# Sums of blocks of g by adding DMA transfers, and seven-segment products for the first pair of units

## Chip, cores and metric

The kernel runs on one core of a Trainium2 chip. The metric is the device time of one execution in microseconds (us). The engines are PE (TensorE, matrix products), DVE (VectorE), ACT (ScalarE), POOL (GpSimd) and SP (SyncE, which here only issues transfers). Each has its own queue and works through it in order; a DMA transfer is issued by an engine's queue and then runs on its own.

## The reference

A Mamba-2 scan is followed by a two-layer feed-forward block. Only what the change touches is given in full.

```python
# scan: x (4, 8, 768, 32), a (4, 8, 768), B and C (4, 8, 768, 16) -> attn_out (4, 8, 768, 32)
...
x = np.ascontiguousarray(attn_out.transpose(0, 2, 1, 3)).reshape(B * S, H * D)   # (3072, 256)
h = x @ w_in                              # w_in (256, 2048)
g = h * (1.0 / (1.0 + np.exp(-h)))        # silu
return (g @ w_out).astype(np.float32)     # w_out (2048, 256), result (3072, 256)
```

All is in 32-bit floats. The weights come as 64-bit floats and are converted on the chip.

## The kernel before

**Units and pairs.** The 3072 tokens are 12 units of 256. Two units make a pair, P = 0 to 5. For each unit the scan yields XM, the unit's x; the first product and silu yield g (tile gT, in the dictionary GTS, 128 partitions by 16 blocks of 256 tokens); the second product yields the output.

**Products by seven.** From pair 2 on, the first product of two units (f_x1) is made with seven multiplications of blocks in the place of eight (the Strassen-Winograd scheme). It needs sums of blocks of the weights (SW, made by f_SW) and of x (XT, made by f_XT). From pair 1 on, the second product (s2_pair) is made so too: seven segments named 1, w, 5, 6, 7, 4, 3, each of eight matmuls that add up in one bank of PSUM (o_ps), with sums of blocks of w_out (SO, made by f_SO on DVE) and of g (f_TS). The sums of g come in four steps, i = 0 to 3: step 0 writes the tile TN, steps 2, 1 and 3 overwrite blocks b12, b11 and b21 of g in place. Here b12 is the first half of d_ff of the pair's second unit, and so on. Step 1 uses the result of step 2, and step 3 that of step 1. Each step is eight operations of 128x256 on POOL (on DVE in part for the last pair). When a segment ends, ACT copies o_ps into a tile ps; POOL adds ps tiles (p_add); DVE transposes the result and SP issues its four output transfers (f_out). The ps_o pool has one buffer, so the next segment's first matmul waits for ACT's copy.

**Units 0 to 3, and the old list.** In the first product units 0 to 3 are computed directly by f_s1, eight rounds of four matmuls each. In the second product units 0 and 1 are computed directly by s2_list: per unit 32 matmuls.

**The order.** It is written out by hand. Each engine's queue follows the order in which the Python code calls. After the start-up, a stage of eight rounds runs f_s1 for unit 2 with four matmuls of the second product of unit 0 behind each round (f_s2(4)), and then a stage for unit 3 with those of unit 1. The names used later:

- *Pieces.* Weights are converted in 16 pieces, 0 to 7 of w_in and 8 to 15 of w_out: ACT (w_size), DVE (three operations) and POOL (L182, in w_bits). Pieces 13, 14 and 15 are made in rounds 0 to 2 of unit 2's stage ("late").
- *Scan of a unit*, spread over the rounds by scan_piece: P (prefix products, DVE), E (a scan, DVE), T (transposes, DVE), B and C (POOL), G (PE; it needs B), S and M (DVE, after G), SM (ACT, after S), Y (PE) and X (ACT copies the result into XM).
- *Loads of a unit* (load_unit): 17 transfers issued by SP. In unit 3's stage, rounds 2 and 5 issue those of units 6 and 7.
- *Stages of seven products*, G = 2 to 5: eight rounds of f_x1(G), each with the scan of the units two further on and seven matmuls of s2_pair(G - 1). ORDER is a hand-written string for each round: W, 1, 5, 6, 7, 4, 3 are first-product matmuls, s is one second-product matmul. Segment 5 of round 0 needs the first of the four XT differences, which POOL makes (f_XT) at the end of the stage before.
- *Tail.* After stage 5 the second product of the last pair stands alone, s2_pair(5, True).

Of the kernel before, what the change touches and what calls it, by code (L numbers as in the profile page):

```python
# [21 lines left out]
def kernel(  # L22
# [22 lines left out]
    nc = tc.nc  # L45
# [425 lines left out]


    def f_s1(g, j):
        if j == 0:
            GTS[g] = gpool.tile([128, NF, UT], FP32, name="gT")
# [7 lines left out]
        nc.scalar.activation(GTS[g][:, 2 * j:2 * j + 2], hp, AF.Silu)  # L483
# [3 lines left out]

    def s2_list(units):
        for g in units:
            b, t0 = at(g)  # L490
            r = out[b * S + t0:b * S + t0 + UT].rearrange("(k c i) m -> k i c m", k=2, c=2)
            o = ps_o.tile([128, 2, d_model], FP32, name="o_ps")
            for c in range(2):
                for f in range(NF):
                    nc.tensor.matmul(out=o[:, c], lhsT=GTS[g][:, f, 128 * c:128 * c + 128], rhs=w_out_sb[:, f, :],  # L495
                                     start=(f == 0), stop=(f == NF - 1), skip_group_check=True)
                    if f == NF - 1 and c == 1:
                        for e in range(2):
                            o_sb = ppool.tile([128, UT], FP32, name="ps")
                            nc.scalar.activation(o_sb, o[:, e], AF.Copy)  # L500
                            for k in range(2):
                                nc.sync.dma_start(out=r[k][:, e], in_=o_sb[64 * k:64 * k + 64])
                    yield
# [6 lines left out]
    def f_SO(i):  # L510
# [4 lines left out]
        def new():  # L515
            if i == 3:
                return lo(spare(None, 128))
            return [wtp.tile([128, 2, WF], FP32, name=n).rearrange("p a (b m) -> p (a b) m", m=128)
                    for n in ("wu", "wv")]
# [3 lines left out]
        a0, a1, op = ((b(0, 1), b(1, 1), ALU.add), (SO[0], b(0, 0), ALU.subtract),  # L523
                      (b(0, 0), b(0, 1), ALU.subtract), (b(1, 0), SO[min(i, 1)], ALU.subtract))[i]
# [3 lines left out]
    def gb(P, k, v):  # L528

        return GTS[2 * P + v].rearrange("p (j k) t -> p k j t", k=2)[:, k]  # L530

    def f_TS(P, i, q, engine):


        if i == 0 and q == 0:
            TN[P] = tpool.tile([128, NF // 2, UT], FP32, name="TN")
        b11, b21, b12, b22 = gb(P, 0, 0), gb(P, 1, 0), gb(P, 0, 1), gb(P, 1, 1)
        o, a0, a1 = ((TN[P], b12, b11), (b11, b22, TN[P]), (b12, b22, b12), (b21, b21, b11))[i]
        for j in (2 * q, 2 * q + 1):
            engine.tensor_tensor(out=o[:, j], in0=a0[:, j], in1=a1[:, j], op=ALU.subtract)  # L540
# [389 lines left out]
```

## Time and profile before

| What | Value |
|---|---|
| Median of 3 runs | 359.7 us (359.67 to 360.05) |
| Profiled execution: its own time | 358.11 us |
| Profiled execution: span from first to last instruction | 356.3 us |
| PE busy | 344.3 us, 97% of the span |
| DVE, ACT, POOL busy | 183.2, 160.7, 181.9 us |
| PE line L572 (second product by seven), share of the ending chain | 30% in o_ps, 3% in hp |
| PE line L495 (old list) | 128 records, 30.9 us |
| POOL line L540 (f_TS) | 72 + 40 + 32 operations of about 0.745 us |
| POOL line L627 (f_SW) | 4 operations of about 2.35 us |

A 32-bit matmul appears in the trace as two records, so 128 records are 64 matmuls. A busy time of a group is the time in which at least one of its records ran. L is a line of the kernel before. The time of the execution is 1.8 us longer than its span, for what lies ahead of the first and behind the last instruction.

### The profile page before, as it was taken

The numbers are of one execution on the slowest core, as the hardware profiler recorded it, in microseconds if no ns is written. First come the engines' busy times: TensorE is split into PE (matmuls) and PEld (weight loads), VectorE is DVE, ScalarE is ACT, GpSimd is POOL, SyncE is SP. The second block draws the span as 40 slices with busy tenths as digits, with TensorE's granted clock in tenths as the row PEclk, the third lists the DMA queues.
The fourth block names the chain that finished last, engine by engine and source line by source line (L and its number), as shares of the span: only waits on it lengthen the run. The fifth ranks groups of instructions, "written<-read, shape, count | busy, mean of one in ns | idle before, by whom it ended". The sixth has DMA issues, their size and how long they took to land.

```text
span 356.3 us, 8309 instructions
## 1 busy us (share of the span) xinstructions
PE 344.3 (97%) x3276; PEld 289.0 (81%) x3277; DVE 183.2 (51%) x389; ACT 160.7 (45%) x390; POOL 181.9 (51%) x246
## 2 busy tenths in 40 slices
PE   7879999999999999999999999999999999999994
PEld 2457888888888888888888888888888888888883
DVE  7978999554447444643454633455632221214722
ACT  2649575223222545545544545544545454453100
POOL 4434345524059076498274398264398930596100
PEclk9999999999999999999999999999999999999998
DMA  6898966871455270161026253110001010001203
GB/s 118 211 338 139 328 192 113 139 115 50 99 109 76 63 110 7 46 110 29 15 53 108 44 99 42 16 18 2 15 2 18 15 17 0 15 2 20 40 2 45
DMA packets 110059, 26.53 MB, mean 74 GB/s; under 512 B 98884, under 2 KB 105796, under 8 KB 110020
## 3 DMA queue, kind: packets, MB, share of 16 engines
q1 hardware_dynamic: 107044, 25.67, 35.5%
q10 hardware_dynamic: 2976, 0.33, 0.6%
q8 instruction: 26, 0.43, 0.5%
q14 instruction: 13, 0.11, 0.1%
HBM read 22.83 MB, written 3.15 MB: 73 GB/s over the span
## 4 chain that ended last, share of the span: by engine, by line
PE 91%; DVE 4%; DMA 2%; issue 1%; POOL 0%; SPq 0%; ACT 0%; ACTq 0%; DVEq 0%
PE o_ps L572 30%; PE hp L655 28%; PE hp L481 15%; PE o_ps L495 8%; PE hp L572 3%; PE gy L461 3%; PE gy L452 2%; PE gy L398 2%; DVE E L297 1%; PE gy L383 1%; DVE wv L178 1%; DMA tbc<-in_C_dram 1%; DMA tbc<-in_B_dram 1%; DMA out_dram<-ot 0%; DVE gT L273 0%
## 5 line engine op out<-in xcount | busy, mean ns | idle before, releaser
L658 DVE TENSOR_TENSOR gT<-hp,p 128x256 f32<-128x256 f32 x64 | 26.9, 420 | 84.6 <-ACT p L669 47.5
L481 PE MATMUL hp<-XM,w_in_sb 128*128 128x256 f32 x256 | 59.4, 381 | 1.9 <-POOL w_in_sb L182 1.1
L661 ACT ACTIVATE gT<-gT 128x256 f32<-128x256 f32 x96 | 39.7, 413 | 42.8 <-DVE gT L658 42.8
L334 POOL TENSOR_TENSOR BT<-bn,E 128x256 f32<-128x256 f32 x12 | 9.0, 751 | 94.5 <-PE hp L655 29.6
L572 PE MATMUL o_ps<-gT,w_out_sb 128*128 128x256 f32 x224 | 56.5, 379 | 0.0
L481 PEld LDWEIGHTS hp<-XM,w_in_sb 128*128 128x128 f32 x256 | 48.0, 190 | 9.7 <-POOL w_in_sb L182 2.4
L655 PE MATMUL hp<-raw 128*128 128x256 f32 x192 | 52.7, 380 | 0.0
L540 POOL TENSOR_TENSOR gT<-gT 128x256 f32<-128x256 f32 x72 | 51.3, 745 | 0.0
L572 PEld LDWEIGHTS o_ps<-gT,w_out_sb 128*128 128x128 f32 x224 | 42.4, 190 | 5.9
L655 PEld LDWEIGHTS hp<-raw 128*128 128x128 f32 x192 | 36.2, 190 | 5.4 <-POOL ps L543 0.6
L483 ACT ACTIVATE gT<-hp 128x512 f32<-128x512 f32 x32 | 19.1, 596 | 40.1 <-PE hp L481 40.1
L669 ACT ACTIVATE p<-hp 128x256 f32<-128x256 f32 x64 | 24.6, 384 | 27.5 <-PE hp L655 25.7
L658 DVE TENSOR_TENSOR gT<-hp,u 128x256 f32<-128x256 f32 x32 | 13.6, 424 | 40.8 <-PE hp L655 40.8
L655 PE MATMUL hp<-XM,w_in_sb 128*128 128x256 f32 x128 | 34.1, 389 | 0.0
L543 POOL TENSOR_TENSOR ps<-ps 128x256 f32<-128x256 f32 x28 | 20.4, 729 | 26.0 <-ACT ps L579 12.7
L495 PE MATMUL o_ps<-w_out_sb,gT 128*128 128x256 f32 x128 | 30.9, 384 | 0.0
L540 POOL TENSOR_TENSOR TN<-gT 128x256 f32<-128x256 f32 x40 | 28.8, 745 | 0.0
L495 PEld LDWEIGHTS o_ps<-w_out_sb,gT 128*128 128x128 f32 x128 | 23.8, 190 | 3.8 <-issue 0.5
L655 PEld LDWEIGHTS hp<-XM,w_in_sb 128*128 128x128 f32 x128 | 23.3, 190 | 4.3 <-issue 1.0
L297 DVE TENSOR_TENSOR_SCAN E<-ab,diag 128x256 f32<-128x256 f32 (+1 forms) x32 | 24.5, 804 | 3.7 <-PE gy L461 3.4
L540 POOL TENSOR_TENSOR gT<-gT,TN 128x256 f32<-128x256 f32 x32 | 22.2, 743 | 0.0
L579 ACT ACTIVATE ps<-o_ps 128x256 f32<-128x256 f32 x31 | 11.9, 384 | 18.5 <-PE o_ps L572 18.1
(121 smaller groups left out, 543.0 us busy)
## 6 DMA issues: line engine op xcount, KB each, us to landing
ab<-in_a_dram SPq DMA_DIRECT2D x40, 128.0 KB, 3.7
raw<-in_moe_w_in_dram SPq DMA_DIRECT2D x8, 512.0 KB, 8.1
raw<-in_moe_w_out_dram SPq DMA_DIRECT2D x8, 512.0 KB, 6.5
xt<-in_x_dram SPq DMA_DIRECT2D x24, 128.0 KB, 4.1
out_dram<-ot SPq DMA_DIRECT2D x76, 32.0 KB, 1.7
bn<-in_B_dram SPq DMA_DIRECT2D x22, 64.0 KB, 5.1
tbc<-in_C_dram SPq DMA_DIRECT2D x40, 32.0 KB, 2.1
pa<-in_a_dram SPq DMA_DIRECT2D x10, 128.0 KB
```

Of the source, the lines that this page charges most:

```text
L297: nc.vector.tensor_tensor_scan(out=E[u].rearrange("p k h t -> p (k h t)")[:, Q * g0:Q * (g0 + n)], data0=t.rearrange("p g t -> p (g t)"), ...
L481: nc.tensor.matmul(out=hp[:, i], lhsT=w_in_sb[:, kc, f * 128:(f + 1) * 128], rhs=xm[:, kc], start=(kc == 0), stop=(kc == KC - 1))
L483: nc.scalar.activation(GTS[g][:, 2 * j:2 * j + 2], hp, AF.Silu)
L495: nc.tensor.matmul(out=o[:, c], lhsT=GTS[g][:, f, 128 * c:128 * c + 128], rhs=w_out_sb[:, f, :], start=(f == 0), stop=(f == NF - 1), skip_ ...
L540: engine.tensor_tensor(out=o[:, j], in0=a0[:, j], in1=a1[:, j], op=ALU.subtract)
L543: engine.tensor_tensor(out=o, in0=p, in1=q, op=ALU.add)
L572: nc.tensor.matmul(out=o, lhsT=w(j), rhs=g()[:, j], start=(j == 0), stop=(j == NF // 2 - 1))
L579: nc.scalar.activation(pn, on, AF.Copy)
L655: nc.tensor.matmul(out=o, lhsT=w, rhs=x_, start=start, stop=True, skip_group_check=True)
L658: nc.vector.tensor_tensor(out=o, in0=p, in1=q, op=ALU.add)
L661: nc.scalar.activation(o, i, AF.Silu)
L669: nc.scalar.activation(o, i, AF.Copy)
```

## The change

1. *Sums of g's blocks.* g's tile is laid out so that each half of d_ff is contiguous in a partition. Most steps of f_TS become DMA transfers issued by POOL that add to their destination, two halves of 128x1024 (512 KB) per step. TN is first filled by a plain transfer that SP issues (f_TN). All steps are additions now; signs in SO and in the output sums change accordingly. In the tail, DVE and POOL make the second half of steps 0 and 2, and DVE makes steps 1 and 3, in operations of 128x1024.
2. *Pair 0.* s2_list is gone. Pair 0 uses s2_pair with joint=True: its segments 1 and w run together, block by block, in the two halves of one o_ps tile, and then 5, 6, 7, 4 and 3 follow. The rounds of the two stages run 4, 4, 4, 4, 3, 3, 3, 3 and 4, 3, 4, 3, 4, 3, 4, 3 of its 56 matmuls. Pair 0's outputs now go through p_add, transposes and f_out in these stages.
3. *Weight sums.* f_SW runs on DVE, no longer on POOL; f_SO and f_SW stand at other rounds.

The core of the diff (new functions in full):

```diff
+    def new_g():
+        return gpool.tile([128, NF, UT], FP32, name="gT").rearrange("p (k j) t -> p k j t", k=2)
...
-        nc.scalar.activation(GTS[g][:, 2 * j:2 * j + 2], hp, AF.Silu)
+        nc.scalar.activation(GTS[g][:, :, j], hp, AF.Silu)
...
-        a0, a1, op = ((b(0, 1), b(1, 1), ALU.add), (SO[0], b(0, 0), ALU.subtract),
-                      (b(0, 0), b(0, 1), ALU.subtract), (b(1, 0), SO[min(i, 1)], ALU.subtract))[i]
+        a0, a1, op = ((b(0, 1), b(1, 1), ALU.subtract), (SO[0], b(0, 0), ALU.subtract),
+                      (b(0, 0), b(0, 1), ALU.subtract), (b(1, 0), SO[min(i, 1)], ALU.add))[i]
...
+    def f_TN(P, h):
+        if h == 0:
             TN[P] = tpool.tile([128, NF // 2, UT], FP32, name="TN")
+        js = slice(4 * h, 4 * h + 4)
+        nc.sync.dma_start(out=TN[P][:, js], in_=gb(P, 0, 1)[:, js])
+
+    def f_TS(P, i, h, engine=None):
         b11, b21, b12, b22 = gb(P, 0, 0), gb(P, 1, 0), gb(P, 0, 1), gb(P, 1, 1)
-        o, a0, a1 = ((TN[P], b12, b11), (b11, b22, TN[P]), (b12, b22, b12), (b21, b21, b11))[i]
-        for j in (2 * q, 2 * q + 1):
-            engine.tensor_tensor(out=o[:, j], in0=a0[:, j], in1=a1[:, j], op=ALU.subtract)
+        js = slice(4 * h, 4 * h + 4)
+        o, a = ((TN[P], b11), (b11, b12), (b12, b22), (b21, b11))[i]
+        if engine is None:
+            nc.gpsimd.dma_start(out=o[:, js], in_=a[:, js], accum_op=ALU.add)
+        elif i == 0:
+            engine.tensor_tensor(out=o[:, js], in0=a[:, js], in1=b12[:, js], op=ALU.add)
+        else:
+            engine.tensor_tensor(out=o[:, js], in0=a[:, js], in1=o[:, js], op=ALU.add)
...
+        if joint:
+            o = ps_o.tile([128, 2, UT], FP32, name="o_ps")
+            for j in range(NF // 2):
+                for n, (m, w, g) in enumerate(segs[:2]):
+                    nc.tensor.matmul(out=o[:, n], lhsT=w(j), rhs=g()[:, j], start=(j == 0 and n == 0), stop=(j == last),
+                                     skip_group_check=True)
...
-        nc.gpsimd.tensor_tensor(out=t, in0=a0, in1=a1, op=op)
+        nc.vector.tensor_tensor(out=t, in0=a0, in1=a1, op=op)
...
-    S2.append(s2_list((0, 1)))
+    for h in range(2):
+        f_TN(0, h)
+        f_TS(0, 0, h)
+    S2.append(s2_pair(0, joint=True))
     for j in range(8):
+        waiting, PEND[:] = PEND[:], []
         f_s1(2, j)
-        scan_piece(3, j, ("", "", "T", "E", "BS", "G", "S", "Y"))
-        f_s2(4)
+        f_s2(4 if j < 4 else 3)
         if j < len(late):
             w_steps(late[j])
+        scan_piece(3, j, ("", "", "T", "OE", "DCO", "G", "OS", "Y"))
+        outputs(waiting)
         if j in (2, 5):
             load_unit(4 + j // 3)
...
+        for h in range(2):
+            if j in (0, 4, 6):
+                f_TS(0, {0: 2, 4: 1, 6: 3}[j], h)
     for j in range(8):
+        waiting, PEND[:] = PEND[:], []
         f_s1(3, j)
-        scan_piece(4, j, ("TE", "BS", "G", "Y", "", "", "", ""))
-        scan_piece(5, j, ("", "", "T", "E", "BS", "G", "Y", ""))
+        scan_piece(4, j, ("TE", "DCS", "G", "YO", "", "", "", ""))
+        scan_piece(5, j, ("", "", "T", "E", "DCS", "G", "YS", ""))
         scan_piece(6, j, ("",) * 7 + ("t",))
-        f_s2(4)
+        f_s2(4 - j % 2)
+        outputs(waiting)
         if j in (2, 5):
             load_unit(6 + j // 3)
-        if j in (1, 4, 6, 7):
-            f_SO(len(SO))
+        if j == 5:
+            f_TN(1, 0)
+            f_TS(1, 0, 0)
+            f_TS(1, 2, 0)
         if j == 7:
             for i in range(4):
                 f_XT(2, i)
-        if j == 5:
-            sums(1, (0, 1))
     for G in range(2, NU // 2):
         S2.append(s2_pair(G - 1))
...
+        f_TN(G - 1, 1)
         for j, (dve, act, pe) in enumerate(plan):
...
+            if j == 0:
+                f_TS(G - 1, 0, 1)
+                f_TS(G - 1, 2, 1)
+            if j == 1 or j == 3:
+                for h in range(2):
+                    f_TS(G - 1, j, h)
+            if j == 5:
+                f_TN(G, 0)
+                f_TS(G, 0, 0)
+                f_TS(G, 2, 0)
             if j == 6 and more:
                 for i in range(4):
                     f_XT(G + 1, i)
...
     P = NU // 2 - 1
-    sums(P, (3,))
+    f_TS(P, 0, 1, nc.vector)
+    f_TS(P, 2, 1, nc.gpsimd)
...
-            for q in range(4):
-                f_TS(P, 2 * n + 1, q, nc.vector)
+            for h in range(2):
+                f_TS(P, 2 * n + 1, h, nc.vector)
```

"D" and "C" in the new strings are B and C of the scan called singly, "O" is f_SO, "S" is f_SW. outputs calls the output steps that the round before left waiting.

## The prediction

> **What bounds the kernel now.** First the page: busy time, the slices, the chain that ended last. Then one window over PE from its last start-up gap to its last matmul.
>
> ```profile
> PE 344.3 (97%) x3276; PEld 289.0 (81%) x3277; DVE 183.2 (51%) x389; ACT 160.7 (45%) x390; POOL 181.9 (51%) x246
> PE   7879999999999999999999999999999999999994
> PE 91%; DVE 4%; DMA 2%; issue 1%; POOL 0%; SPq 0%; ACT 0%; ACTq 0%; DVEq 0%
> ```
> ```profile
> 27.65:351.40 323.75, 323.75 (x2916) 277.16 (x2916) 160.42 (x340) 148.24 (x366) 170.78 (x223) 1.00 0.33 62
> ```
>
> From 27.65 to 351.40 us PE is busy for all of its 323.75 us. So every matmul removed there is worth its pitch, and every new wait of PE costs its whole length. POOL and DVE are half idle: what they lose or gain counts only where PE, directly or through POOL's or SP's queue, waits for it. The stage that changes most is 55.15 to 116.97 (units 2 and 3 in the first product, 0 and 1 in the second). Its queues, in the timeline by engine:
>
> ```profile
> 113.52 1.89 PE L481 MATMUL hp<-XM,w_in_sb 128*128 128x256 f32 x8
> 115.24 1.89 PE L495 MATMUL o_ps<-w_out_sb,gT 128*128 128x256 f32 x8
> 116.97 1.03 PE L655 MATMUL hp<-XM,w_in_sb 128*128 128x256 f32 x4
> ```
> ```profile
> 57.70 1.38 POOL L182 TENSOR_TENSOR w_out_sb<-wu,wv 128x512 uint32<-128x512 uint32 x1 [0.97 <-DVE wv L178]
> 60.04 1.27 POOL L182 TENSOR_TENSOR w_out_sb<-wu,wv 128x512 uint32<-128x512 uint32 x1 [0.96 <-DVE wv L178]
> 62.74 1.27 POOL L182 TENSOR_TENSOR w_out_sb<-wu,wv 128x512 uint32<-128x512 uint32 x1 [1.42 <-DVE wv L178]
> ...
> 112.47 0.89 POOL L638 TENSOR_TENSOR raw<-XM 128x256 f32<-128x256 f32 x1 [0.24 <-ACT XM L470]
> ```
> ```profile
> 56.94 0.63 SPq L86 DMA_DIRECT2D pa<-in_a_dram  x1
> ...
> 98.53 0.64 SPq L86 DMA_DIRECT2D pa<-in_a_dram  x1
> 99.21 2.85 SPq L115 DMA_DIRECT2D tbc<-in_B_dram  x4
> 102.11 1.83 SPq L115 DMA_DIRECT2D tbc<-in_C_dram  x4
> 104.04 2.65 SPq L95 DMA_DIRECT2D ab<-in_a_dram  x4
> 106.79 1.19 SPq L107 DMA_DIRECT2D bn<-in_B_dram  x2
> 108.08 1.42 SPq L122 DMA_DIRECT2D xt<-in_x_dram  x2
> ```
>
> To see: eight records (four matmuls) start every 1.73 us, so one matmul costs 0.432 us. The w_out pieces 13, 14 and 15 (57.70, 60.04, 62.74) are done 2.4 to 4.2 us before PE reads them. A unit's loads cost SP about 10 us of issue (98.53 to 109.50: 11.0). The x differences for the next stage (L638) are ready 4.4 us before that stage's first seven-product matmul, at 117.83.
>
> **What the Trainium skill says.** "DMA: Bandwidth & Descriptors", section "Anatomy of one DMA — SWDGE (gpsimd) path": about 2.0 us plus bytes/436e3, so for 512 KB an estimated 3.2 us; a semaphore wait happens on the issuing sequencer before dispatch. The profile has 6.5 to 8.1 us for the 512 KB weight loads, with others in flight. The same page, "Latency and other measured facts": a DMA issued from GpSimd (POOL) needs about 1 us to its first byte; I take that as POOL's time per issue. The kernel before has none. "Collectives: The Full Stack", "The bandwidth ceiling: the fold count and why AG ≠ RS ≠ AR": an adding transfer pays for two source reads, not for the add; so I estimate 2.0 + 2 x 1.2 = 4.4 us for 512 KB. Not shown by this trace either. "SBUF — State Buffer", "Who interferes with whom": a DVE operation with two SBUF inputs and a reading GpSimd one exclude each other. The trace agrees: L526 on 128x512 takes 0.67 us alone, 1.13 to 1.21 us beside POOL.
>
> **Part by part.**
>
> 1. *Seven segments for units 0 and 1.* 64 matmuls become 56: 8 x 0.432 = 3.45 us less on PE, all on the path.
>
> 2. *Bank changes.* The pair's o_ps has one buffer. The old list changed it only between rounds. Now segments change inside a run of second-product matmuls three times (5 to 6, 7 to 4, 4 to 3). Evacuation starts 0.04 us after the last matmul's end (83.90, ACT L500 at 83.94), takes 0.384 us (L579), and the next matmul starts some 0.1 us later (estimate): against a pitch of 0.216 after a start, 0.379 + 0.04 + 0.384 + 0.1 leaves 0.7 us lost each. At 7 to 4 ACT first copies XM (0.6 us, after Y): 0.8. At 4 to 3 ACT first runs SM of unit 5, which ends 1.7 us after G (73.53 to 75.28 in unit 3's case), while PE reaches the change 0.86 us after G: 1.3. The first, 5 to 6, is in point 4.
>
> 3. *w_out pieces behind the sums (A).* SP issues the two TN copies where unit 4's loads began, 56.94. With xt ahead of them I put their landing at 61.0 and 62.2 (3.2 us each plus queue). POOL's queue now reads: add into TN half 0, half 1 (each waits for its copy), piece 13, two more adds, pieces 14 and 15. With 1 us per issue: piece 13 done at 64.5, 14 at 67.8, 15 at 69.1. PE wants them at 62.9, then 67.2 and 68.8 in its delayed course: 1.7 + 0.7 + 0.4 = 2.8 us. Bounds: 0.8 (copies by 60.5, issue 0.3) and 6 (weight-load latency).
>
> 4. *First use of a doubly summed block (B).* SO[0] on DVE waits for piece 15; E of unit 3 comes behind it (about 4.7 us), then B and C on POOL (0.7 each), and only then POOL issues b11's add: about 76.2, landed at about 81.1. Segment 6 wants it at 79.7: 1.4 us, the bank change included. Bounds 0.7 and 4.5 (an add of 8 us).
>
> 5. *x differences behind a copy (E).* This is the largest term. In unit 3's round 5 POOL gets the next pair's first adds, ahead of f_XT. They wait for a TN copy on SP, which stands behind unit 7's 17 load issues, and these behind segment 7's output issues, which wait for DVE. From the end of G of unit 4 (T): DVE does S and M (2.6), T (1.1), SO[3] (1.3 to 2.1), P and E0 (1.7), E (2.3), SW[2] (1.2 to 2.0), the transpose (0.4): T+11.4. SP: four output issues 2.5 (L552: 10.25 us for 12 under load, L502: 2.5 for 4), loads 10.0, the copy's issue 0.4: T+24.3; landed T+27.8. POOL: two issues 2.0 (0.6 to 2.4), segment 3's add 0.73, first difference 0.77: T+31.2. PE from T to segment 5 of the next stage: rounds 2 to 7 with points 2's waits, T+24.6. A wait of 6.4 us; bounds 4.3 and 9. Even with SP on time, segment 3's add now stands before f_XT and costs some 1.2 us.
>
> 6. *POOL relieved.* 144 L540 operations (72 + 40 + 32, 102.3 us) and four L627 (9.5 us) leave POOL: nothing for PE, which waited on none of them. In their place stand 42 adds and 11 copies of 512 KB. In the seven-product stages (54 us, eight rounds of 6.7) each sum is due about two rounds after its issue, so 4.4 us hides; it stops hiding at about 10 us. The DMA share there is 0.34, later 0.07; eight adds fit a stage at up to 6.7 us each.
>
> 7. *SW on DVE, SO earlier, signs swapped, g's layout, tail.* DVE is idle for 32% and 51% of the stage's two halves (20.84 busy of 30.69 us, 15.36 of 31.20); beyond points 4 and 5 nothing, and at most the four SW's 5 to 8 us if it were full. In the tail DVE and POOL each do 128x1024 at once (POOL 2.35, L627); segment 5 starts 6.9 us in, the first sums end earlier: nothing. If that cover went, at most 2 us.
>
> Sum: -3.45 + 0.8 + 1.3 + 2.8 + 1.4 + 6.4 = +9.2 us. The profiled execution (span 356.3, its own time 358.1) becomes 365.5 and 367.3; the shown median, 1.6 above that execution, becomes 368.9.
>
> **Rivals.**
>
> - *The wait is not POOL's.* If an adding DMA that waits for its copy waits in the DMA's own queue, the operations behind it on POOL pass: pieces 13 to 15 and the x differences come as before, points 3 and 5 vanish, and three bank changes of 0.7 are left: -3.45 + 2.1 = -1.35, 358.3. For it: PE is full, so a saving can't get lost elsewhere. Against: on SP, output issues held up by DVE do hold what stands behind them (in the waits of SP, L552 behind L550 for 93.7 us), and the skill says the same of any issuer. It decides for "faster" when all waits of PE together stay under 2.7 us. Chance 0.10; a sum near zero 0.03.
> - *Only the short waits.* SP reaches the copy in time (loads cheaper, or DVE's transpose early), leaving E at 1.2 to 2 and A near 1: about +1.7, 361.4. Chance 0.12.
> - *The adding DMAs are slow.* At over 10 us each, B costs 6 and each later stage waits for its sums, four stages of some 3 us: about +25, 385. Nothing in the trace excludes it. Chance 0.08.
> - *My forecast*, 0.67.
>
> **Numbers.** 368.9 us. Range 361 to 376: short waits at the low end; all upper bounds together give +18, which I count half. It leaves out the faster and equal cases (0.13) and the slow adds (0.07). A difference under 0.2%, 0.7 us, can't be told from none here. Faster 0.10, same 0.03, slower 0.87.
>
> **What would show it.** Right: gaps of PE at w_out pieces 13 to 15 near 63 to 69 us; PE idle some 6 us at the start of the seven-product stage of units 4 and 5, released by POOL's x differences, with SP's unit 7 loads just before the TN copy; no gaps in later stages. Wrong: no PE gap there, adds landing after more than 10 us, or gaps that recur in every stage.

## The result, and the profile after

The changed kernel takes 375.3 us (median of four runs, 374.8 to 376.0), the kernel before on the same chip 359.9 (359.7 to 360.2). The ratio is 1.043, with a 95% interval of 1.0408 to 1.0451: it is slower, by 15.5 us. The forecast was 368.9, with 361 to 376. The profiled execution has a span of 373.1 us (own time 374.8) against 356.3. Medians in this document are over all runs of a kernel; ratios leave out the few runs that took over 1.5% longer than its fastest.

The page of the kernel after, in the same order as before: busy time, slices of PE and of its clock, and the shares of the chain that ended last.

```profile
PE 348.9 (94%) x3260; PEld 288.9 (77%) x3261; DVE 188.8 (51%) x386; ACT 161.8 (43%) x393; POOL 118.8 (32%) x148
PE   8869999979998189999999999999999999999994
PEclk9998999999999769999999999999999999999999
PE 83%; DMA 4%; DVE 3%; POOL 3%; issue 3%; ACT 1%; SPq 1%; ACTq 0%; DVEq 0%; POOLq 0%
```

A slice is 9.3 us long. PE has one hole in the 14th slice (the digit 1, 121 to 131 us), and the granted clock sinks in the 14th and 15th. The chain no longer runs along PE alone: DMA, POOL and the issues have 10% between them, where DMA and issue had 3%. POOL has become idle, as the change meant it to (181.9 to 118.8 us), and this bought nothing.

The timeline of PE, with the waits in brackets (start, length, line, tiles, number of records, idle time before and what ended it):

```profile
82.61 0.67 PE L615 MATMUL o_ps<-gT,wu 128*128 128x256 f32 x2 [2.19 <-DMA gT<-gT]
...
88.28 1.99 PE L485 MATMUL hp<-XM,w_in_sb 128*128 128x256 f32 x8 [0.69 <-ACT XM L470]
...
103.92 1.13 PE L615 MATMUL o_ps<-gT,w_out_sb 128*128 128x256 f32 x4 [0.47 <-ACT ps L571]
...
113.34 0.70 PE L615 MATMUL o_ps<-gT,raw 128*128 128x256 f32 x2 [1.07 <-ACT ps L571]
...
121.96 1.03 PE L670 MATMUL hp<-XM,w_in_sb 128*128 128x256 f32 x4
131.93 1.22 PE L670 MATMUL hp<-raw 128*128 128x256 f32 x2 [8.93 <-POOL raw L653]
132.94 1.06 PE L615 MATMUL o_ps<-gT,w_out_sb 128*128 128x256 f32 x2
133.79 1.06 PE L670 MATMUL hp<-raw 128*128 128x256 f32 x2
134.64 2.64 PE L615 MATMUL o_ps<-gT,w_out_sb 128*128 128x256 f32 x6
137.12 0.60 PE L670 MATMUL hp<-raw 128*128 128x256 f32 x2
```

From the top: segment 6 waits for b11's adding transfer (point 4, B); unit 3's first product waits for XM(3), which the prediction had not seen; two bank changes wait for ACT's copy (point 2); and the x differences come 8.9 us late (point 5, E). Then look at the starts behind that wait: the twelve records from 131.93 to 137.12 took 5.19 us, 0.43 us each, where at full clock they start every 0.216 us. So the wait cost another 2.6 us after it had ended. A window over this place and one over a later stage (busy time of PE, PEld, DVE, ACT and POOL, granted clock, DMA share, GB/s):

```profile
125.00:140.00 15.00, 8.07 (x26) 6.73 (x27) 1.31 (x6) 2.67 (x7) 6.98 (x9) 0.66 1.03 217
150.00:200.00 50.00, 50.00 (x467) 42.54 (x473) 24.29 (x59) 25.42 (x69) 15.85 (x22) 1.00 0.75 145
```

In the later stages PE is busy all the time, although the DMA share has gone from 0.34 to 0.75. Why E is so late is read from POOL's queue, and from SP's beside it (timelines of the kernel after):

```profile
113.37 1.78 POOL L540 TENSOR_TENSOR ps<-ps 128x256 f32<-128x256 f32 x1 [3.20 <-ACT ps L571]
128.68 0.87 POOL L533 DMA_DIRECT2D TN<-gT  x1 [13.53 <-DMA TN<-gT]
129.26 1.18 POOL L533 DMA_DIRECT2D gT<-gT  x1
129.83 1.37 POOL L540 TENSOR_TENSOR ps<-ps 128x256 f32<-128x256 f32 x1
130.51 1.36 POOL L653 TENSOR_TENSOR raw<-XM 128x256 f32<-128x256 f32 x1
```
```profile
110.48 2.17 SPq L549 DMA_DIRECT2D out_dram<-ot  x4
112.69 0.63 SPq L86 DMA_DIRECT2D pa<-in_a_dram  x1
...
122.32 1.59 SPq L122 DMA_DIRECT2D xt<-in_x_dram  x2
124.09 0.54 SPq L524 DMA_DIRECT2D TN<-gT  x1
```

POOL stands still for 13.5 us at its adding transfer into TN. It waits for the plain copy into TN, which SP issues only at 124.09, behind segment 7's outputs and unit 7's loads. The copy then lands within about 4 us, and the first x difference (L653), for which PE stands, is third in POOL's queue behind it.

To see what belongs to what, each profile is cut at three marks of PE: the first matmul of the second product, the first matmul of the first seven-product stage, and the first matmul of unit 6's G in that stage. (Each is the start of a record in PE's timeline; the last column is the span less the third mark.)

| Kernel | to second product | the two stages | to unit 6's G | rest |
|---|---|---|---|---|
| before | 55.15 | 61.82 | 12.18 | 227.15 |
| after | 57.11 | 64.85 | 23.88 | 227.26 |
| after less before | +1.96 | +3.03 | +11.70 | +0.11 |

The first column is not the change: the instructions of PE ahead of that mark are the same, and the mark lies at 54.7 to 59.7 us over all the profiles of this study. It goes with the granted clock from 28 to 40 us, which differs from run to run: the profiles with 1.00 have the mark at 54.7 to 55.8 us, those with 0.86 to 0.89 at 56.5 to 57.3, those with 0.72 at 59.0 to 59.7. The kernel before varies too (357.4 to 362.8 us over all its runs); that this is the same cause is likely, but only one of its runs has a trace. So 14.8 of the 16.8 us are to be explained: 6.5 us of waits against 3.45 saved in the two stages, and 11.7 us at E.

### The profile page after: what moved, and what is told of

Same layout as the page of the kernel before. It is cut to its first block, busy times and chain, and to the rows that moved or that the text cites. A ratio compares the mean times of both kernels' runs of the same rounds, so it can differ in the third digit from the quotient of the medians.

```text
span 373.1 us, 8278 instructions
## 1 busy us (share of the span) xinstructions
PE 348.9 (94%) x3260; PEld 288.9 (77%) x3261; DVE 188.8 (51%) x386; ACT 161.8 (43%) x393; POOL 118.8 (32%) x148
## 4 chain that ended last, share of the span: by engine, by line
PE 83%; DMA 4%; DVE 3%; POOL 3%; issue 3%; ACT 1%; SPq 1%; ACTq 0%; DVEq 0%; POOLq 0%
PE o_ps L615 33%; PE hp L670 27%; PE hp L485 12%; PE hp L615 3%; PE gy L461 2%; PE gy L398 2%; PE gy L452 2%; DMA gT<-gT 2%; DMA TN<-gT 1%; POOL w_out_sb L182 1%; PE gy L383 1%; POOL TN L533 1%; POOL gT L533 1%; DVE wv L178 1%; DVE E L297 1%
## 5 line engine op out<-in xcount | busy, mean ns | idle before, releaser
L673 DVE TENSOR_TENSOR gT<-hp,p 128x256 f32<-128x256 f32 x64 | 26.9, 421 | 98.4 <-ACT p L684 49.9
L485 PE MATMUL hp<-XM,w_in_sb 128*128 128x256 f32 x256 | 61.2, 389 | 2.7 <-ACT XM L470 1.4
L615 PE MATMUL o_ps<-gT,w_out_sb 128*128 128x256 f32 x240 | 62.3, 388 | 0.5 <-ACT ps L571 0.5
L485 PEld LDWEIGHTS hp<-XM,w_in_sb 128*128 128x128 f32 x256 | 48.9, 194 | 11.2 <-POOL w_in_sb L182 2.4
L540 POOL TENSOR_TENSOR ps<-ps 128x256 f32<-128x256 f32 x35 | 29.2, 833 | 85.8 <-ACT ps L571 76.4
L615 PEld LDWEIGHTS o_ps<-gT,w_out_sb 128*128 128x128 f32 x240 | 46.5, 195 | 7.7 <-ACT ps L571 0.9
L670 PEld LDWEIGHTS hp<-raw 128*128 128x128 f32 x192 | 36.8, 193 | 14.8 <-POOL raw L653 9.3
L533 POOL DMA_DIRECT2D gT<-gT x31 | 30.1, 1030 | 32.2 <-PE hp L670 21.4
L670 PE MATMUL hp<-XM,w_in_sb 128*128 128x256 f32 x128 | 34.1, 389 | 0.0
L615 PE MATMUL o_ps<-gT,wu 128*128 128x256 f32 x88 | 22.6, 381 | 2.2 <-DMA gT<-gT 2.2
L571 ACT ACTIVATE ps<-o_ps 128x256 f32<-128x256 f32 x38 | 14.5, 384 | 22.2 <-PE o_ps L615 19.7
L615 PE MATMUL o_ps<-gT,wv 128*128 128x256 f32 x88 | 22.4, 380 | 0.0
L615 PE MATMUL o_ps<-gT,raw 128*128 128x256 f32 x80 | 20.6, 382 | 1.1 <-ACT ps L571 1.1
L533 POOL DMA_DIRECT2D TN<-gT x11 | 9.7, 885 | 33.6 <-DMA TN<-gT 30.3
```

What stands on the lines that cost most here:

```text
L485: nc.tensor.matmul(out=hp[:, i], lhsT=w_in_sb[:, kc, f * 128:(f + 1) * 128], rhs=xm[:, kc], start=(kc == 0), stop=(kc == KC - 1))
L533: nc.gpsimd.dma_start(out=o[:, js], in_=a[:, js], accum_op=ALU.add)
L540: engine.tensor_tensor(out=o, in0=p, in1=q, op=op)
L571: nc.scalar.activation(pn, on, AF.Copy)
L615: nc.tensor.matmul(out=o, lhsT=w(j), rhs=g()[:, j], start=(j == 0), stop=(j == last))
L670: nc.tensor.matmul(out=o, lhsT=w, rhs=x_, start=start, stop=True, skip_group_check=True)
```

## Experiments

All start from the changed kernel. Each was timed beside the kernel before on the same chip. First the table, with the same cuts as above, then one by one. The cuts in a row are those of one profiled run, which is not always near the median (e3's took 375.4 us, e8's 363.0, e12's 368.4).

| Kernel | median us | ratio to before (95%) | to second product | two stages | to unit 6's G | rest |
|---|---|---|---|---|---|---|
| e1 | 369.6 | 1.026 (1.016 to 1.035) | 55.17 | 68.47 | 12.70 | 229.06 |
| e2 | 367.4 | 1.019 (1.011 to 1.026) | 55.03 | 69.26 | 13.99 | 227.12 |
| e3 | 372.4 | 1.034 (1.028 to 1.041) | 55.77 | 70.06 | 20.81 | 227.06 |
| e4 | 375.3 | 1.045 (1.039 to 1.051) | 54.70 | 69.97 | 21.22 | 227.01 |
| e5 | 370.8 | 1.032 (1.027 to 1.036) | 57.07 | 61.44 | 22.38 | 230.11 |
| e6 | 373.1 | 1.041 (1.037 to 1.045) | 57.17 | 60.38 | 26.85 | 227.00 |
| e7 | 368.5 | 1.026 (1.024 to 1.029) | 56.48 | 62.28 | 20.46 | 227.08 |
| e8 | 360.7 | 1.003 (1.001 to 1.005) | 58.98 | 62.58 | 12.18 | 227.56 |
| e9 | 370.6 | 1.031 (1.028 to 1.034) | 59.09 | 67.66 | 14.61 | 228.64 |
| e10 | 366.1 | 1.020 (1.016 to 1.025) | 57.30 | 60.74 | 17.69 | 228.67 |
| e11 | 361.4 | 1.005 (1.001 to 1.009) | 56.53 | 61.74 | 13.38 | 227.25 |
| e12 | 365.0 | 1.017 (1.013 to 1.020) | 59.72 | 65.48 | 14.22 | 227.18 |

**e1_xt_first: the x differences ahead of the next pair's sums on POOL.**

```diff
-        if j == 5:
+        if j == 6:
+            for i in range(4):
+                f_XT(2, i)
             f_TN(1, 0)
             f_TS(1, 0, 0)
             f_TS(1, 2, 0)
-        if j == 7:
-            for i in range(4):
-                f_XT(2, i)
```

> The changed kernel with one edit: in unit 3's stage the four x differences stand in round 6, ahead of pair 1's first TN copy and adds. Queue theory (PE waited 8.93 us for the first difference because POOL held it behind an add that waited for a copy which SP issued late): the wait at the start of the stage of units 4 and 5 goes entirely, with the slower clock behind it (5.19 us for 12 matmul records instead of 2.6), so 11.5 us less than the changed kernel's 375.3, near 363.8. Rival (the adding transfers themselves are what costs, wherever they stand): at most 3 us less, above 372, and the pair's later sums make PE wait instead.

The wait for the x differences is gone: the stretch to unit 6's G takes 12.70 us, 11.2 less than in the changed kernel. But the median fell by 5.7 us only, half of what was expected. What is late next is a sum, in the timeline of PE of e1:

```profile
149.21 1.10 PE L615 MATMUL o_ps<-gT,wu 128*128 128x256 f32 x4 [1.04 <-DMA gT<-gT]
```

The two stages, however, took 68.5 us and not 64.9. Here PE came to the second product 1.9 us earlier than in the profile of the changed kernel, so it waited 2.44 us for piece 13 (0.18 there). The matmuls after that wait ran at half the clock (eight records in 3.4 us, a loss of 1.6). The short A of the changed kernel was thus a piece of luck: the late start hid it (A is 2.4 to 2.9 us for piece 13 in e1, e2 and e3, which all came to the second product by 55.8 us).

**e2_tn_before_loads: only SP's order.**

```diff
         if j in (2, 5):
+            if j == 5:
+                f_TN(1, 0)
             load_unit(6 + j // 3)
         if j == 5:
-            f_TN(1, 0)
             f_TS(1, 0, 0)
```

> The changed kernel with one edit: SP issues pair 1's first TN copy ahead of unit 7's 17 loads; POOL's order stays. Queue theory, in its form that SP's order is the cause: the copy is issued about 11.4 us earlier (112.7 in place of 124.1), it lands near 117, and only the floor stays, the add of segment 3 ahead of the first difference, about 1.3 us of PE; so 9 to 10.5 us less, near 365.5. If SP's order were not the cause (the copy slow by itself, or POOL's two issues of 0.9 us): less than 3 us gained, above 372.

The waits of PE in e2:

```profile
PE o_ps L601 <- POOL w_out_sb L182: 2.6, 1, 2.6
PE o_ps L615 <- DMA gT<-gT: 2.5, 1, 2.5
...
PE hp L670 <- POOL raw L653: 1.2, 1, 1.2
```

The wait for POOL's first x difference fell from 8.9 to 1.2 us, with POOL's order unchanged. So the late place of one SP issue was needed for it, and by e1 POOL's order was needed too. A and B stay (2.6 and 2.5 us), and the median is 1.9 us above the expectation.

**e3_pe_warm: the clock.** Twenty matmuls whose result nobody uses are put into the wait.

```diff
+                if G == 2 and j == 0:
+                    d = ps_o.tile([128, 2, UT], FP32, name="o_ps")[:, 0]
+                    for _ in range(20):
+                        mm(d, wj[:, 0, 0, 0], b0[:, 0])
```

> The changed kernel with 20 extra matmuls (8.6 us) on PE in the place where it waited for the first x difference; their result is not used. If the slow 12 records after the wait (5.19 us, granted clock 0.66 in the window from 125 to 140) come from PE's having been idle, the clock stays at 1.0 and the kernel gains 2.0 to 2.6 us, near 373. If the clock falls for another reason (transfers, load of the other engines), no change within 0.5 us, or 0.5 us more where the extra matmuls run over.

The timeline of PE of e3 at that place:

```profile
126.69 8.80 PE L670 MATMUL o_ps<-XM,w_in_sb 128*128 128x256 f32 x40
135.32 0.59 PE L670 MATMUL hp<-raw 128*128 128x256 f32 x2
135.76 0.59 PE L615 MATMUL o_ps<-gT,w_out_sb 128*128 128x256 f32 x2
136.19 0.59 PE L670 MATMUL hp<-raw 128*128 128x256 f32 x2
136.62 1.46 PE L615 MATMUL o_ps<-gT,w_out_sb 128*128 128x256 f32 x6
137.91 0.59 PE L670 MATMUL hp<-raw 128*128 128x256 f32 x2
```

The stretch without useful work is only 0.5 us shorter (PE does nothing useful until 135.32), but the same twelve records now take 2.59 us and not 5.19. The stretch to unit 6's G shrinks by 3.1 us, the median by 2.9. The low clock is a consequence of PE's idleness, not of the transfers that run at the time.

**e4_pieces_first: pair 0's TN copies, and the sums of its steps 0 and 2, behind piece 15.**

```diff
-    for h in range(2):
-        f_TN(0, h)
-        f_TS(0, 0, h)
...
+        if j == 2:
+            for i in (0, 2):
+                for h in range(2):
+                    if i == 0:
+                        f_TN(0, h)
+                    f_TS(0, i, h)
```

> The changed kernel with one edit: pair 0's TN copies, its adds into TN and those of step 2 stand behind the last piece of w_out (round 2 of unit 2's stage) in POOL's queue. Queue theory: the pieces come as in the kernel before, PE's two waits there (1.2 us) go; the chain from piece 15 over SO[0], E, B and C to b11's add begins 3 us earlier, so segment 6's wait of 2.2 us shrinks to the bank change; together 2 to 3 us less, but the later wait at the x differences grows by part of it, since SP's lag doesn't move; so 373 to 375. Rival (the copies and adds slow other transfers): the same stage isn't shorter, no change.

A is gone. But the sums come later, and the gain is handed on: B, which was expected to shrink, grows to 4.8 us, and E is still 7.3. The waits of PE in e4:

```profile
PE hp L670 <- POOL raw L653: 7.3, 1, 7.3
PE o_ps L615 <- DMA gT<-gT: 4.8, 1, 4.8
```

**e5_combined: e4's late sums (with the TN copies early on SP), segments that end with a round, XM(3) earlier, e2's and e1's orders, all at once.**

```diff
+        if j == 7:
+            f_Y(3)
+            f_X(3)
-        f_s2(4 if j < 4 else 3)
+        f_s2(4 if j < 4 else 2)
...
-        f_s2(4 - j % 2)
+        f_s2(4)
```

> All four orders at once: pieces 13 to 15 ahead of pair 0's adds on POOL, with the two TN copies issued early on SP; segments 5, 6, 7, 4, 3 of units 0 and 1 end with a round (2 products a round in the second half of unit 2, 4 in unit 3's rounds); in unit 2's last round the scan's products and the XM copy stand before the second product; TN's first copy for the next pair ahead of unit 7's loads, and the x differences ahead of the next pair's adds. If queue order alone lost the time: no wait of PE over 1 us left between the second product's start and its end except the one short wait for XM, the two stages 52 to 53 us long against 55.3 before, and in all 356 to 358 us, below the kernel before by 1.5 to 3.5 (3.45 of it the eight matmuls). If the adding transfers themselves cost something that no order takes away (landing time, a lower clock, slower neighbours), new waits for g's blocks appear in place of the old ones and the time stays at 361 to 366, near that of the run that only moved TN's copy.

The two stages now take 61.44 us, and no wait over 0.5 us is left in them but 1.9 us for unit 5's B. (The expectation's 52 to 53 us, against 55.3 before, was a slip: the two stages before take 61.82.) Still the kernel is 11 us slower than the one before, where 1.5 to 3.5 us less were expected. In the timelines of POOL and PE of e5:

```profile
138.41 0.87 POOL L533 DMA_DIRECT2D TN<-gT  x1 [15.50 <-DMA TN<-gT]
```
```profile
140.89 0.69 PE L383 MATMUL gy<-xt,BT 64*32 64x64 f32 x32 [10.13 <-POOL BT L334]
```

It is the same wait, one station on. The first copy into TN now passes unit 7's loads, but the second (f_TN(1, 1), at the start of the next stage) stands behind them on SP, issued at 135.02. POOL waits for it 15.5 us, and unit 6's B stands behind POOL's adding transfer. The theory that one displaced issue was the whole of E held for e1 and e2, where PE passed the place later, and fell here.

**e6_bank_ends: only the bank changes and XM(3).** The three edits shown at e5, nothing else.

> Only the bank changes and the XM copy are mended: segments end with a round, the XM copy of unit 3 comes before the last second product of the round. The two evacuation waits (0.5 and 1.1 us) go, the XM wait of 0.7 goes, and segment 6 starts about 1.7 us later against its add, so B falls from 2.4 to 0.7 or less. If the wait for the x differences is anchored in SP's and DVE's queues as in the prediction's point 5, PE only comes to it earlier: it grows by most of what was saved, to 10 to 13 us, and the time stays within 2 us of the changed kernel, 373.5 to 376. If the waits are independent, the savings add up: 370 to 371.

The two stages fell from 64.85 to 60.38 us, with every wait but A's remainder gone. And the wait for the x differences grew, as the first of the two expectations had it. PE's and SP's timelines of e6:

```profile
131.18 1.22 PE L670 MATMUL hp<-raw 128*128 128x256 f32 x2 [12.61 <-POOL raw L653]
```
```profile
123.38 0.54 SPq L524 DMA_DIRECT2D TN<-gT  x1
```

PE arrives 4.4 us earlier (117.55), SP issues the copy 0.7 us earlier, and PE goes on 0.75 us earlier. What is saved ahead of a wait whose end hangs on another queue comes back in that wait: 4.5 us of saving, 2.3 us of it in the median. The one for B is seen too: segment 6 begins two rounds later against its add, and no longer waits.

**e7_plain_copies: no add in the transfers.** The sums of g are left out of the computation.

```diff
-            nc.gpsimd.dma_start(out=o[:, js], in_=a[:, js], accum_op=ALU.add)
+            nc.gpsimd.dma_start(out=o[:, js], in_=a[:, js])
```

> The transfers of the sums carry no add: plain copies from the same places to the same places in the same order; the sums are left out of the computation. If the adding makes a transfer slow (two reads for each byte written), the transfers land in about 4.0 to 4.5 us instead of 7.0, the wait of segment 6 shrinks from 2.4 to under 1 us, and the wait for the x differences, which hangs on the TN copy's place behind unit 7's loads, stays at 7.5 to 9: 371.5 to 374 us. If the landing time is that of the route from block to block and of the queue, it stays near 7 us and the time at 375. If adding transfers were the source of the whole loss, it would come near 360.

From issue to landing, the transfers of POOL's line L533, first in the kernel after, then in e7:

```profile
DMA to landing us min/median/max: 4.6/6.6/10.7
```
```profile
DMA to landing us min/median/max: 2.8/4.2/8.0
```

The add costs 2.4 us of a transfer's 6.6, and 0.3 us of POOL's time to issue it (medians 0.87 and 0.53). B falls from 2.2 to 0.7 us. E falls to 6.2 us, more than expected, and the median is 6.9 us below the changed kernel, 3 below the expected range. SP's timeline shows why E fell: unit 4's loads took 15.2 us to issue and not 21.7, so that SP was at segment 7's outputs before DVE had transposed them. From the end of unit 4's G its copy issue ended after 24.8 us and not 26.9, and POOL got from the copy's landing to the first difference in 2.8 us and not 3.5. But 9.0 us over the kernel before are left without any add: the plain transfers and the order of the queues are still there.

**e8_halves_for_0_1: one part alone.** Units 0 and 1 keep the old list (here on the new layout of g), all else as changed: 25 adding transfers into g, and TN's nine copies and nine adds, remain for the later pairs, and f_SW runs on DVE.

```diff
-    for h in range(2):
-        f_TN(0, h)
-        f_TS(0, 0, h)
-    S2.append(s2_pair(0, joint=True))
+    S2.append(s2_list((0, 1)))
...
-        f_s2(4 if j < 4 else 3)
+        f_s2(4)
```

> One part alone: units 0 and 1 keep the second product in halves (64 matmuls, no sums, no TN copy, no bank changes for them), while the later pairs' sums come by adding transfers and the weight sums on VectorE as in the changed kernel. By the prediction's points: no -3.45, and A, B, C and D go; of E there stays what POOL's queue makes by itself. SP has no output of segments to wait for (four plain output issues in its place) but still unit 7's 17 issues ahead of the TN copy: the wait for the x differences falls from 8.9 to 2 to 6 us, in all 361 to 367. If the whole loss comes from the seven segments of units 0 and 1, 359 to 360.5; if it comes from the adding transfers as such, 370 or more.

The median is 360.7 us, a ratio of 1.003 (1.001 to 1.005). The stretch to unit 6's G takes 12.18 us, to the hundredth what it takes in the kernel before. In the two stages 0.76 us are lost. The waits of PE in e8 name it, the second XM wait of 0.7 us, since f_s2 still stands ahead of the scan:

```profile
PE hp L485 <- ACT XM L470: 1.4, 2, 0.7
```

So the adding transfers in the later stages and the weight sums on DVE cost next to nothing (0.4 us in the last column). Nearly the whole loss comes with the seven segments for units 0 and 1: in part from their bank changes (2.1 us, point 2), mostly from what they put into SP's and POOL's queues. My expectation had left 2 to 6 us at E here. I had put unit 7's loads down as the cause, and they are still ahead of the TN copy in e8. SP's and DVE's timelines of the kernel after, then SP's of e8:

```profile
65.55 6.96 SPq L95 DMA_DIRECT2D ab<-in_a_dram  x4
```
```profile
108.95 0.43 DVE L547 STREAM_TRANSPOSE ot<-ps 128x256 f32<-128x256 f32 x1
```
```profile
61.27 2.67 SPq L95 DMA_DIRECT2D ab<-in_a_dram  x4
...
112.53 0.69 SPq L524 DMA_DIRECT2D TN<-gT  x1
```

In e8 POOL still stands at the copy, for 8.4 us, but the copy is issued 9.0 us before PE begins the next stage; in the changed kernel it is issued 2.1 us after. Two things ahead of it differ. Segment 7's outputs stand before unit 7's loads, and DVE ends their transpose only at 109.38 us. And SP is late by itself: while pair 0's copies and adds ran, unit 4's loads took 21.7 us to issue (58.46 to 80.17), against 11.2 in e8 and 10.4 in the kernel before. SP had no pause after that and came to these outputs at 110.48, 1.1 us after the transpose. Had it been early, it would have waited for the transpose, so the slow issues cost only this 1.1 us of the copy's place (an estimate from these times). Why the issues were slow is not shown.

**e9_copies_on_act: all TN copies issued by ACT, which writes their source.**

```diff
-        nc.sync.dma_start(out=TN[P][:, js], in_=gb(P, 0, 1)[:, js])
+        nc.scalar.dma_start(out=TN[P][:, js], in_=gb(P, 0, 1)[:, js])
```

> One edit to the changed kernel: all eleven TN copies are issued by ACT, which has written their source, in place of SP, where they stand behind a unit's loads and the outputs. If the place in SP's queue made the wait for the x differences (8.9 us, and the lower clock after it, 2.6), both go, POOL's wait for a TN copy falls from 13.5 us to the landing of about 4 to 5 us, and what stays are the waits of the middle: pieces 13 to 15 up to 2.6, segment 6 2.4, XM 0.7, two evacuations 1.5, less the eight matmuls: 361 to 365 us, some 11 less than the changed kernel. If the wait comes from the landing of transfers on full DMA queues, POOL still waits over 8 us and the time stays above 370. ACT's issues may cost PE up to 0.5 us each where ACT feeds the seven products: if more than that, waits for ACT's copies appear in every seven-product stage.

E is down to 1.2 us, and the stretch to unit 6's G to 14.61. But the median is 370.6 us, 4.7 less than in the changed kernel where some 11 were expected. The gain is half lost elsewhere: ACT issued pair 0's copies 2.5 us after PE's first matmul of the second product, where SP did so within 0.1 us, so piece 13 stood behind the adds into TN for longer on POOL and A became 3.8 us. In the stage of units 4 and 5 PE waited 0.8 us for an ACT copy behind such an issue.

**e10_combined_on_act: e5 with e9's edit.**

> The combined order of e5_combined with the TN copies issued by ACT. In e5_combined the profile shows the same wait one station on: POOL stands 15.5 us at the adding transfer of TN's second half, whose copy is behind unit 7's loads on SP, and unit 6's B behind it on POOL (PE waits 10.1 us), then a lowered clock. If that is all, both go: no wait of PE over 2 us after 30 us, 355 to 358 us, below the kernel before by 2 to 4. If something else in the adding transfers costs (their landing of 7 us, the load on the DMA engines), a wait of 2 to 6 us for g's blocks or for a unit's loads comes up in its place: 359 to 363.

The 10 us wait for B is gone; one of 2.0 us at segment 5 and one of 3.5 at the x differences stay, and the median of 366.1 us lies above both expectations. ACT's queue in e10:

```profile
116.42 0.47 ACTq L524 DMA_DIRECT2D TN<-gT  x1
...
122.43 0.51 ACTq L524 DMA_DIRECT2D TN<-gT  x1
```

ACT had been free since 110.2 us, but the first copy was issued at 116.4, and XM's copy behind it at 117.4. The trace's semaphores show what it waited for: in this program the transfers of SP and ACT share eight counters of completion, taken in turn, and each transfer waits for the one that had its counter before. For this copy that was a load of unit 7, which SP issued at 114.45 and which landed at 116.32; for the second copy a load that landed at 122.36. So another engine's queue did not free the copies of SP's.

**e11_tn_on_pool: no copies.** e5's order, and POOL forms TN itself in operations of 128x1024.

```diff
     def f_TN(P, h):
         if h == 0:
             TN[P] = tpool.tile([128, NF // 2, UT], FP32, name="TN")
-        js = slice(4 * h, 4 * h + 4)
-        nc.sync.dma_start(out=TN[P][:, js], in_=gb(P, 0, 1)[:, js])
...
+        if engine is None and i == 0:
+            engine = nc.gpsimd
         if engine is None:
```

> The combined order of e5_combined, and no TN copies any more: POOL forms TN's halves itself (128x1024, some 2.35 us each, in place of two transfers with a copy and an add), all other sums stay adding transfers; the x differences stand ahead of the next pair's sums. In e10 the copies still waited on ACT for a transfer eight issues earlier in the program, a load of unit 7 on SP (issued at 116.4 and 122.4 us where ACT was free at 110), and held POOL for 8.0 us and ACT's XM copy, so PE for 3.5. If the copies' place behind SP's issues is the whole of E, no wait of PE over 1 us stays after 45 us, the two stages take 60.4 to 61.5 us (61.8 before, 64.9 in the changed kernel, 60.7 in e10), and the time is 356.5 to 359.5, at or up to 3 us below the kernel before. If POOL's longer sums bring a new wait (2.35 us where an issue took 1), it shows at segment 5, or at unit 6's and 7's B, with 1 to 4 us: 360 to 363.

The median is 361.4 us, a ratio of 1.005 (1.001 to 1.009): all but 1.6 us of the loss is gone, and E with it. So the seven segments for units 0 and 1 can stay: with e5's orders, the transfers into TN made nearly all of what was left (e5: 370.8 us). The time is in the range of the second expectation, but the new wait is at another place: 3.1 us for unit 3's B, and one of 1.0. POOL's and DVE's timelines of e11 show its origin:

```profile
65.13 5.57 POOL L535 TENSOR_TENSOR TN<-gT 128x1024 f32<-128x1024 f32 x2
```
```profile
65.65 2.84 DVE L513 TENSOR_TENSOR wv<-w_out_sb 128x512 f32<-128x512 f32 x1
68.42 2.43 DVE L278 TENSOR_SCALAR pz<-pa 128x256 f32<-128x256 f32 x1
```

L513 takes 0.67 us elsewhere and L278 0.28. Beside a POOL operation with two operands in SBUF, which took 2.8 us here, each of these two DVE operations lasted nearly as long as that operation.

**e12_tn_in_quarters: the same in operations of 128x256, and the second half of pair 0's TN two rounds later.**

```diff
+            n = 1 if engine is nc.gpsimd else 4
+            for j in range(4 * h, 4 * h + 4, n):
+                engine.tensor_tensor(out=o[:, j:j + n], in0=a[:, j:j + n], in1=b12[:, j:j + n], op=ALU.add)
...
-        for i in {2: (0, 2), 4: (1,), 6: (3,)}.get(j, ()):
-            for h in range(2):
-                f_TS(0, i, h)
+        for i, h in {2: ((0, 0), (2, 0)), 4: ((0, 1), (2, 1), (1, 0), (1, 1)), 6: ((3, 0), (3, 1))}.get(j, ()):
+            f_TS(0, i, h)
```

> As e11_tn_on_pool, with POOL's TN sums cut into operations of 128x256 (0.7 us each, four for a half), and units 0 and 1's second half of TN formed two rounds later, after unit 3's B. In e11 one POOL operation of 128x1024 (2.35 to 2.8 us) held single DVE operations for its whole length: DVE's negated decays took 2.43 and 3.28 us where they take 0.28, SO's second half 2.84 where it takes 0.67; so unit 3's E and B came late (PE waits 3.1) and a sum of the seven products too (1.0). If that exclusion is the cause, no DVE operation there takes over 1.5 us, both waits go, and the time is 356.5 to 359, below the kernel before by 1 to 3. If POOL's work itself is too much at that place, B of unit 3 still makes PE wait 2 to 3 us, or segment 6 waits for b11's sum, and the time stays at 360.5 to 362.

The median is 365.0 us, above both expectations. The trace of e12 is that of its longest run, so only its queues are read here. DVE's, POOL's and PE's timelines:

```profile
70.00 0.81 DVE L278 TENSOR_SCALAR pz<-pa 128x256 f32<-128x256 f32 x1
...
127.02 4.13 DVE L278 TENSOR_SCALAR pz<-pa 128x256 f32<-128x256 f32 x1
```
```profile
127.95 3.04 POOL L537 TENSOR_TENSOR TN<-gT 128x256 f32<-128x256 f32 x4
```
```profile
90.72 3.75 PE L617 MATMUL o_ps<-gT,wu 128*128 128x256 f32 x8 [3.62 <-DMA gT<-gT]
...
132.34 0.67 PE L672 MATMUL hp<-raw,w_in_sb 128*128 128x256 f32 x2 [1.80 <-DVE gT L675]
```

At the first place L278 takes 0.81 us and the wait for unit 3's B is 0.28, as the exclusion would have it; but the second half of TN was moved behind that B as well, and the two edits were not separated. In the next stage, where nothing was moved, the smaller operations did not help: L278 took 4.13 us, longer than the 3.28 of e11, until an addition and four quarters had run one behind the other on POOL, and PE waited 1.8 us for a sum behind it (1.0 in e11). Cutting a POOL operation into pieces that follow each other without a pause did not let DVE in between there. And the second half of the sums now comes too late for segment 6: PE waits 3.6 us, with half clock after it (eight records in 3.5 us). That this is what makes the shorter runs of e12 slower than e11 is likely, but they have no trace. No version tried here is faster than the kernel before.

## Why the prediction was right, and where its sum was off

The direction and the place were right: SP's unit 7 loads ahead of the TN copy, POOL standing at its adding transfer, the x differences behind it, PE idle at the start of the stage of units 4 and 5, and no wait in the later stages. e1 and e2 show that mechanism by taking away one order each. The forecast was 6.4 us too low, and A, which came out 1.6 us under its forecast by the luck of the late start, hid some of what was missing. Term by term, with the profile of the changed kernel:

| Point | forecast | measured | |
|---|---|---|---|
| 1 eight matmuls | -3.45 | -3.45 by count | given back in the waits |
| 2 bank change 7 to 4, 4 to 3 | 0.8, 1.3 | 0.74, 1.34 | right |
| 3 A, pieces 13 to 15 | 2.8 | 1.23 | 2.4 to 2.9 for piece 13 alone in e1 to e3 |
| 4 B, segment 6 | 1.4 | 2.35 | |
| - XM(3) behind f_s2 | none | 0.9 | missed |
| 5 E, x differences | 6.4 | 8.9 | |
| - clock after E | none | 2.6 | missed |
| 6, 7 later stages, tail | 0 | 0.1 | right |
| - start-up | none | 2.0 | not the change |

- *Point 4* was mis-sized in the landing of an adding transfer. The prediction took 4.4 us for 512 KB, from the rule of two source reads that it cites, and 4.9 with the issue in the chain; b11's took 6.0 (issued at 76.55, landed near 82.5), and the median of all is 6.6. e7 shows that the add costs something beyond a plain transfer (4.2 us without it), but it costs 2.4 us and not the 1.2 of the estimate, and the plain level is higher than estimated too. The page that the prediction cites says it of the adds in collectives; that a second read is the reason here is not shown.
- *Point 5* was mis-sized along the whole chain. From the end of unit 4's G (97.7 us), SP's copy issue ended at 26.9 us and not at 24.3; unit 7's loads cost 11.2 us of issue and not 10.0, and the outputs ahead of them ended 1.1 us late. The first difference ended 34.2 us after G, not 31.2: 2.6 us of this stand at the copy's issue already, 0.3 came with its landing (3.8 us behind the issue, at 128.39), and POOL's issues and additions took 3.5 us, about as forecast. PE was there 0.7 us later than forecast.
- *A wait's length was taken for its whole cost.* This is the step that failed in kind. "TensorE: Matmul & The Clock Gate", Part 1, in the Trainium skill says that the clock falls to half after an idle window of about 3.4 us, and that the window runs freely. The trace agrees in the half clock: behind E the records start every 0.43 us in place of 0.216, 2.6 us in all, and e3 shows that the idleness is its cause. It does not agree in the length: waits of 2.4 to 3.0 us were already followed by half clock in e1, e2 and e3, and the measurement decides.
- *XM(3)* was missed because the diff moves f_s2 ahead of scan_piece. The prediction followed the new queues of POOL, DVE and SP, but not PE's own. e6 and e8 show it: with Y and X ahead of f_s2 the wait of 0.7 us is gone, without that it stays.
- *Point 6*: the adding transfers in the later stages are hidden, as said. e8 shows it best, and says more than the prediction did: apart from pair 0 the change is within 0.1 to 0.5% of the kernel before.
- *The rivals.* That a waiting adding transfer lets POOL pass is refuted by POOL's 13.5 us. "Only the short waits" is what e2 looks like at E (1.2 us), though not at A and B. "The adding DMAs are slow" is not the case: the median landed after 6.6 us, the slowest after 10.7, and no later stage waited.

What stays open: why SP's issues are slow beside pair 0's copies and adds (unit 4's loads: 21.7 us in the changed kernel, 15.2 with plain transfers in e7, 11.2 without any in e8), and how much of e12's wait for segment 6 came from the quarters and how much from the two rounds.

## What to carry to other kernels

A transfer inherits the place of its issue: count everything ahead of it on the issuing engine's queue, with output stores that another engine has to finish first, and everything behind whoever waits for it, before its bandwidth matters. Where the end of a wait hangs on another queue, time saved ahead of it comes back in it (e6), and taking it away uncovers the next one on the same queue (e5). Price an idle gap of the matrix engine at its length plus the slow clock that may follow.

## What the runs showed of the hardware

- **After gaps of 2.4 to 3.2 us the clock fell in some cases and not in others.** Some waits of PE were followed by 1.6 to 1.8 us of loss at half clock (2.44 in e1, 2.50 in e2, 3.03 in e3), others by none (2.49 in e1, 2.87 in e3, 3.14 in e11). At 3.49 (e10) it cost 1.6, at 8.93 in the changed kernel 2.6.
- **An adding transfer of 512 KB between tiles in SBUF landed after 6.6 us** (4.6 to 10.7), a plain one after 4.2 us (2.8 to 8.0), and its issue took POOL 0.87 us against 0.53 (medians).
- **POOL operations on two SBUF operands held single DVE operations for their whole length**: 2.43 us where 0.28 is usual, beside POOL's 128x1024 in e11. Beside operations of 128x256 in e12 the same DVE operation took 0.81 us at one place and 4.13 at another, where five POOL operations followed each other without a pause.
- **SP's issues took longer beside other transfers**: 17 loads of a unit 10.4 us in the kernel before, 21.7 in the changed kernel while 512 KB copies and adds ran.
